# Weight conversion in a pooled-attention and two-MLP kernel: float64 weights turned into two float32 words in 512-word blocks beside the attention, split once and kept

## The chip, the cores and the metric

The kernel runs on one core of a Trainium2 chip. The metric is device time in microseconds (us), the median of several executions; lower is better. The engines are PE (TensorE; PEld is its weight load), DVE (VectorE), ACT (ScalarE) and POOL (GpSimd), which compute, and SP (SyncE), which issues every DMA of this kernel. Each engine works through its own queue in order, so an instruction that waits holds up all that stand behind it on that engine.

## The reference

```python
def _attn_ref(q, k, v):                       # [4, 8, 1152, 64] float32
    q_pool = q.reshape(B, H, S // 2, 2, D).mean(axis=3)
    scores = np.matmul(q_pool, k.transpose(0, 1, 3, 2)) / np.sqrt(D)
    attn = np.exp(scores - np.max(scores, axis=-1, keepdims=True))
    attn = attn / (np.sum(attn, axis=-1, keepdims=True) + 1e-09)
    return np.matmul(attn, v).astype(np.float32)

x = attention output as [2304, 512]           # 4 batches of 576 tokens
h = x @ w_in;  x = np.maximum(0.01 * h, h) @ w_out                      # layer 0
h = x @ w_in2; out = np.where(h > 0, h, np.exp(np.minimum(h, 0)) - 1) @ w_out2   # layer 1
```

`w_in` is [512, 2048] and `w_out` [2048, 512]. The weights arrive as float64, eight bytes each in DRAM; only the results are float32.

## The kernel before, in words

Every float32 operand of a matmul is split into a high word h, rounded to the type that PE multiplies at full rate, and a low word l = x - h; a product is then three matmuls (hh, hl, lh). The helper `psplit` (L258) issues such a split as one instruction for h (L261 on ACT or L263 on DVE) and one subtraction for l (L267 on POOL or DVE).

Attention goes through 16 pairs of heads, four to a batch, nine score tiles to a pair (`attn_pair`). One tile is three 128x384 matmul groups, each followed by one maximum on DVE (L457), so a batch has 108 of these maxima; they serve below as a clock that counts how far the attention has come. Then come exp on ACT (L463), transposes on PE (L475), splits (L261 on ACT, L267 on DVE) and the product with v (L496).

`mlp` does one layer for one batch. For each of 16 feature blocks f it makes h for 128 features (L629, 24 matmuls), the activation on ACT and DVE and a split of the result g (ACT, POOL), and after each four blocks the second product into the accumulators (L667). `load_w` provides the weights of block f as tiles `wi` (3 buffers) and `wo` (6 buffers), each with h and l.

A weight block is 128x512 values, one for `w_in` and one for `w_out` for each f: 64 blocks over both layers. For the first batch of a layer `convert` (L271) makes float32 from the float64 bit pattern in two halves of 256: a load into `cr` (L290), two bit operations on DVE (L293, L296), two conversions on ACT (L299, L301), an addition on POOL (L303) and a last multiplication with a test on DVE (L305) into `wr`. The float32 block is also written to DRAM (L328). For the other three batches `wr` is loaded from that copy (L323). In all four batches `wr` is then split into `wi` or `wo` by ACT (L261) and POOL (L267): 256 splits in all. Waiting for a free `wi` or `wo` happens in ACT's queue.

The order on the engines is set by a list scheduler in the program (`Program.schedule`): every piece of work has an engine, a cost in ns, a rank (the position in the plan; the attention of one tile is one rank, a batch is 36) and its dependences; of what is ready the lowest rank goes first, and the instructions are emitted in the order of the planned starts. `PLAN` gives the rank at which each (batch, layer) MLP starts: 36 and 54 for the first batch, so its MLPs run beside the attention of the second batch, and so on; the last two run with no attention beside them.

## Time and profile before

| | |
|---|---|
| median of 3 runs | 1545.24 us (1543.69 to 1549.79) |
| the profiled execution: its time, its span | 1545.34 us, 1543.5 us |
| PE busy | 92% of the span, 10288 matmuls |
| DVE, ACT, POOL busy | 66%, 69%, 54% |
| DMA | 135.59 MB, 28% of the 16 DMA engines' time |
| granted PE clock | 0.99 of full speed over the span |

The span is what the profile covers; the 1.8 us beside it are outside. Shares are averages over stages with different limits, so each stage is read by itself.

### The profile page before, as it was taken

Reading aid. Unit: us, or ns where it says so; the run is one execution under the profiler, and the core shown is the slowest. Engines: PE = TensorE matmul, PEld = TensorE weight load, DVE = VectorE, ACT = ScalarE, POOL = GpSimd, SP = SyncE. Lnnn points to the kernel's source line nnn. Section 1 sums busy time; section 2 is a strip of 40 time slices with the busy share of each in tenths; the row PEclk is TensorE's granted clock in tenths of the full one; section 3 lists DMA queues with packets and bytes.
Section 4 is the critical chain, followed back from the end, with each engine's and each line's share of the span. In section 5 each row is a group of like instructions: output and inputs, shape, how many; then the busy total and the mean of one; then the engine's idle time right before and its main releaser. Section 6 shows DMA issues by size and latency. Waiting matters only on the chain.

```text
span 1543.5 us, 28953 instructions
## 1 busy us (share of the span) xinstructions
PE 1414.5 (92%) x10288; PEld 1365.2 (88%) x10288; DVE 1011.4 (66%) x2273; ACT 1065.9 (69%) x2901; POOL 830.3 (54%) x840
## 2 busy tenths in 40 slices
PE   5878889888888898999999999999999999899997
...
DVE  6999889899998998556565556645665554124222
...
GB/s 138 99 115 87 40 75 123 121 130 125 126 118 144 130 143 120 74 71 73 67 69 86 79 78 63 74 76 66 71 67 59 55 56 56 93 76 82 69 82 39
DMA packets 82642, 135.59 MB, mean 88 GB/s; under 512 B 8512, under 2 KB 26944, under 8 KB 82496
## 3 DMA queue, kind: packets, MB, share of 16 engines
...
q14 instruction: 65, 0.53, 0.1%
...
## 4 chain that ended last, share of the span: by engine, by line
PE 64%; DVE 21%; ACT 6%; issue 3%; DMA 3%; POOL 2%; SPq 0%; ACTq 0%; POOLq 0%; DVEq 0%
PE h L667 17%; PE h L629 16%; PE s L452 8%; PE o L496 7%; PE t L475 5%; DVE m L457 3%; PE s L629 3%; DVE ct L293 3%; DVE wr L305 3%; DVE ct L296 3%; DVE pt L267 2%; PE s L667 2%; PE t L373 2%; PE t L629 2%; PE t L667 2%
## 5 line engine op out<-in xcount | busy, mean ns | idle before, releaser
L667 PE MATMUL h<-g,wo 128*128 128x288 f32 x2544 | 437.1, 302 | 17.5 <-DVE t L650 7.9
L629 PE MATMUL h<-xs,wi 128*128 128x288 f32 x2520 | 429.2, 305 | 22.9 <-DVE t L650 14.2
L629 PEld LDWEIGHTS h<-xs,wi 128*128 128x128 f32 x2520 | 362.5, 190 | 32.5 <-DVE t L650 20.0
L667 PEld LDWEIGHTS h<-g,wo 128*128 128x128 f32 x2544 | 367.1, 188 | 23.8 <-DVE t L650 9.6
L457 DVE TENSOR_REDUCE m<-s 128x1 f32<-128x384 f32 x432 | 232.2, 550 | 74.4 <-PE s L452 71.6
L261 ACT ACTIVATE pt<-t 128x384 fp32r<-128x384 f32 (+1 forms) x416 | 184.0, 457 | 115.2 <-PE t L475 108.3
L463 ACT ACTIVATE p<-s,m 128x384 f32<-128x384 f32 x432 | 249.5, 588 | 18.3 <-DVE m L459 18.0
L267 DVE TENSOR_TENSOR pt<-t,pt 128x384 fp32r<-128x384 f32 (+1 forms) x416 | 206.8, 509 | 73.3 <-ACT pt L261 71.7
L267 POOL TENSOR_TENSOR g<-t,g 128x288 fp32r<-128x288 f32 x256 | 211.1, 831 | 79.9 <-ACT g L261 75.5
L267 POOL TENSOR_TENSOR wo<-wr,wo 128x512 fp32r<-128x512 f32 x128 | 166.4, 1304 | 137.5 <-ACT wo L261 134.3
L452 PE MATMUL s<-kT,qT 128*128 128x384 f32 x768 | 197.0, 354 | 25.4 <-ACT p L463 24.5
L267 POOL TENSOR_TENSOR wi<-wr,wi 128x512 fp32r<-128x512 f32 x128 | 167.6, 1309 | 91.9 <-ACT wi L261 79.3
L496 PE MATMUL o<-pt,vn 128*128 128x256 f32 (+1 forms) x1152 | 192.5, 303 | 5.5 <-DVE pt L267 3.6
L475 PE MATMUL t<-ident,p 128*128 128x128 f32 x1116 | 181.6, 277 | 12.4 <-DVE pt L267 11.7
L496 PEld LDWEIGHTS o<-pt,vn 128*128 128x128 f32 x1152 | 165.5, 190 | 10.6 <-DVE pt L267 10.2
L475 PEld LDWEIGHTS t<-ident,p 128*128 128x128 f32 x1116 | 139.4, 142 | 22.1 <-DVE pt L267 12.3
L452 PEld LDWEIGHTS s<-kT,qT 128*128 128x128 f32 x768 | 125.5, 192 | 32.2 <-ACT p L463 31.0
L303 POOL TENSOR_TENSOR ct<-ct,cr 128x256 uint32<-128x256 uint32 x128 | 98.8, 774 | 96.7 <-DVE ct L296 29.8
L261 ACT ACTIVATE g<-t 128x288 fp32r<-128x288 f32 x256 | 112.2, 445 | 49.0 <-DVE t L650 28.4
L267 POOL TENSOR_TENSOR vn<-raw,vn 128x576 fp32r<-128x576 f32 x32 | 46.4, 1449 | 174.4 <-ACT vn L261 174.4
L261 ACT ACTIVATE wo<-wr 128x512 fp32r<-128x512 f32 x128 | 80.6, 630 | 78.9 <-PE h L667 47.5
L680 DVE TENSOR_TENSOR acc<-h,acc 128x288 f32<-128x288 f32 x158 | 71.1, 452 | 67.2 <-PE h L667 66.1
(106 smaller groups left out, 2080.0 us busy)
## 6 DMA issues: line engine op xcount, KB each, us to landing
wr<-w SPq DMA_DIRECT2D x192, 256.0 KB, 2.6
cr<-in_moe_w_in_dram SPq DMA_DIRECT2D x64, 256.0 KB, 2.7
cr<-in_moe_w_out_dram SPq DMA_DIRECT2D x64, 256.0 KB, 2.7
w<-wr SPq DMA_DIRECT2D x64, 256.0 KB, 2.4
raw<-in_k_dram SPq DMA_DIRECT2D x32, 288.0 KB, 3.0
raw<-in_v_dram SPq DMA_DIRECT2D x32, 288.0 KB, 3.1
raw<-in_q_dram SPq DMA_DIRECT2D x32, 256.0 KB, 2.9
out_dram<-cr SPq DMA_DIRECT2D x16, 256.0 KB, 2.1
```

Of the source, the lines that this page charges most:

```text
L261: prog.add("ACT", act(n, sbuf=not psum), rank, lambda: A.activation(out=hi(), in_=src(), func=ACTF.Copy), w=[w], r=r)
L267: lambda: eng.tensor_tensor(out=lo(), in0=src(), in1=f32(hi()), op=ALU.subtract),
L293: prog.add("DVE", dve(CW, True), rank, lambda r=r, t=t: V.tensor_scalar(out=t.ap, in0=r[:, :, 1], scalar1=3, scalar2=0x3FFFFFF8, op0=ALU.l ...
L303: prog.add("POOL", pool(CW), rank, lambda t=t, r=r: G.tensor_tensor(out=t.ap, in0=t.ap, in1=r[:, :, 0], op=ALU.add), w=[t], r=[t, (r, 0)])
L452: PE.matmul(out=st[:, 0:384], lhsT=qa(a), rhs=kT[:, 384 * c:384 * c + 384], start=(i == 0), stop=(i == len(seq) - 1))
L457: prog.add("DVE", dve(384), rank - LR, lambda st=st, c=c: V.tensor_reduce(out=m[:, c:c + 1], in_=st[:, 0:384], axis=AX.X, op=ALU.max), w=[ ...
L463: prog.add("ACT", act(384, True), rank - LE, lambda c=c: A.activation(out=p[:, 384 * c:384 * c + 384], in_=banks[c][:, 0:384], func=ACTF.E ...
L475: PE.transpose(out=t[:, i, :], in_=p[:, (3 * c + i) * 128:(3 * c + i + 1) * 128], identity=ident)
L496: PE.matmul(out=o[:, 0:n], lhsT=vn[:, c, :], rhs=pt[th][:, a, c % 3, :], start=(c == 3 * ORDER[0] and a == 0), stop=(c == 3 * ORDER[2] + 2 ...
L629: PE.matmul(out=h[:, 0:HB], lhsT=wi[:, a, c, :], rhs=xs[c][:, e, cols], start=(c == 0 and a == 0 and e == 0), stop=(c == DC - 1 and a == 1))
L667: PE.matmul(out=y[:, 0:HB], lhsT=w[f][1][:, a, d * 128:(d + 1) * 128], rhs=g[f][:, e, cols], start=(f % FC == 0 and a == 0 and e == 0), st ...
L680: prog.add("DVE", dve(HB), rank - HURRY, lambda y=y, a_=a_, cols=cols: V.tensor_tensor(out=a_[:, cols], in0=y[:, 0:HB], in1=a_[:, cols], o ...
```

## The change

`convert` works on 512 words at a time, without the `ct` and `cm` tiles: the intermediate words lie in the tile that becomes the result, and the absolute value (L301) is taken in place. A new function `prepare_w` converts one block into `ws` (2 buffers), splits it there once into h (ACT) and l (POOL), and writes both to DRAM, 512 KB a block. `CONV` gives this stream ranks of its own: layer 0 from 14 to 48, layer 1 from 48 to 66. `load_w` no longer computes: `wi` and `wo` are filled by a DMA from the kept h and l, in all four batches, also in the first. The planner's cost of a group of three MLP matmuls rises from 369 to 399. `cr` buffers are 512 words of eight bytes; `store` uses them too. `SPILL` is empty, so the branches that ask for it do nothing; `PLAN`'s new column holds the same 18 as before.

```diff
-    CW = 256
+    CW = 512
     CB = 2
-    CLEAD = 3
     FC = 4
     GB = 5
     WIB = 3
     WOB = 6
-    WRB = 4
+    WSB = 2
+    CONV = ((14, 48), (48, 66))
+    SPILL = ()
...
-    PLAN = ((0, 0, 36, 0), (0, 1, 54, 0), (1, 0, 72, 0), (1, 1, 90, 0),
-            (2, 0, 108, 0), (2, 1, 126, 0), (3, 0, 144, 1), (3, 1, 162, 1))
+    PLAN = ((0, 0, 36, 18, 0), (0, 1, 54, 18, 0), (1, 0, 72, 18, 0), (1, 1, 90, 18, 0),
+            (2, 0, 108, 18, 0), (2, 1, 126, 18, 0), (3, 0, 144, 18, 1), (3, 1, 162, 18, 1))
...
-            t = sb("ct", [128, CW], U32, CB)
-            mag = sb("cm", [128, CW], F32, CB)
+            t = lambda n=n: f32(dst[:, 1, n:n + CW]).bitcast(U32)
...
             prog.add("DVE", dve(CW, True), rank, lambda r=r, t=t: V.tensor_scalar(
-                out=t.ap, in0=r[:, :, 1], scalar1=3, scalar2=0x3FFFFFF8,
-                op0=ALU.logical_shift_left, op1=ALU.bitwise_and), w=[t], r=[(r, 1)])
+                out=t(), in0=r[:, :, 1], scalar1=3, scalar2=0x3FFFFFF8,
+                op0=ALU.logical_shift_left, op1=ALU.bitwise_and), w=[(dst, n)], r=[(r, 1)])
             prog.add("DVE", dve(CW), rank, lambda r=r, t=t: V.scalar_tensor_tensor(
-                out=t.ap, in0=r[:, :, 1], scalar=0xC0000000, in1=t.ap,
-                op0=ALU.bitwise_and, op1=ALU.bitwise_or), w=[t], r=[(r, 1), t])
+                out=t(), in0=r[:, :, 1], scalar=0xC0000000, in1=t(),
+                op0=ALU.bitwise_and, op1=ALU.bitwise_or), w=[(dst, n)], r=[(r, 1), (dst, n)])
             prog.add("ACT", act(CW, sbuf=True), rank, lambda r=r: A.activation(
                 out=r[:, :, 0], in_=r[:, :, 0], func=ACTF.Copy, scale=2.0 ** -29), w=[(r, 0)], r=[(r, 0)])
-            prog.add("ACT", act(CW, sbuf=True), rank, lambda r=r, mag=mag: A.activation(
-                out=mag.ap, in_=r[:, :, 1].bitcast(F32), func=ACTF.Abs), w=[mag], r=[(r, 1)])
+            prog.add("ACT", act(CW, sbuf=True), rank, lambda r=r: A.activation(
+                out=r[:, :, 1].bitcast(F32), in_=r[:, :, 1].bitcast(F32), func=ACTF.Abs),
+                w=[(r, 1)], r=[(r, 1)])
             prog.add("POOL", pool(CW), rank, lambda t=t, r=r: G.tensor_tensor(
-                out=t.ap, in0=t.ap, in1=r[:, :, 0], op=ALU.add), w=[t], r=[t, (r, 0)])
-            prog.add("DVE", dve(CW), rank, lambda n=n, t=t, mag=mag: V.scalar_tensor_tensor(
-                out=dst[:, n:n + CW], in0=mag.ap, scalar=MIN_HI, in1=t.ap.bitcast(F32),
-                op0=ALU.is_ge, op1=ALU.mult), w=[(dst, n)], r=[t, mag])
+                out=t(), in0=t(), in1=r[:, :, 0], op=ALU.add), w=[(dst, n)], r=[(dst, n), (r, 0)])
+            prog.add("DVE", dve(CW), rank, lambda t=t, r=r: V.scalar_tensor_tensor(
+                out=t().bitcast(F32), in0=r[:, :, 1].bitcast(F32), scalar=MIN_HI, in1=t().bitcast(F32),
+                op0=ALU.is_ge, op1=ALU.mult), w=[(dst, n)], r=[(dst, n), (r, 1)])
...
+    def prepare_w(rank, layer, w_in, w_out, f, i):
+        src = block(layer, w_in, w_out, f, i)
+        ws = sb("ws", [128, 2, 512], F32R, WSB)
+        x = lambda: f32(ws[:, 1])
+            convert(rank, ws, src)
+        prog.add("ACT", act(512, sbuf=True), rank, lambda: A.activation(
+            out=ws[:, 0], in_=x(), func=ACTF.Copy), w=[(ws, "h")], r=[ws])
+        prog.add("POOL", pool(512), rank, lambda: G.tensor_tensor(
+            out=ws[:, 1], in0=x(), in1=f32(ws[:, 0]), op=ALU.subtract), w=[ws], r=[ws])
+        kp = kept[layer, f, i] = Buf(lambda: dram.tile([128, 1024], F32, name=f"w{layer}_{f}_{i}"))
+        prog.add("SP", 60, rank, lambda: nc.sync.dma_start(
+            out=kp.ap, in_=f32(ws.ap).rearrange("p a n -> p (a n)")), w=[kp], r=[ws])
+
     def load_w(rank, layer, w_in, w_out, f):
-
-        src = (w_in[:, f * 128:(f + 1) * 128].rearrange("(c p) f -> p c f", p=128),
-               w_out[f * 128:(f + 1) * 128, :])
-        rs = [sb("wr", [128, 512], F32, WRB) for _ in range(2)]
-        for i, r in enumerate(rs):
-            if w_in.dtype == F32:
-                view = (lambda r=r: r.ap.rearrange("p (c n) -> p c n", c=DC)) if i == 0 else lambda r=r: r.ap
-                prog.add("SP", 60, rank - 1.5, lambda i=i, view=view: nc.sync.dma_start(
-                    out=view(), in_=src[i]), w=[r])
-            elif (layer, f, i) in kept:
-                kp = kept[layer, f, i]
-                prog.add("SP", 60, rank - 1.5, lambda r=r, kp=kp: nc.sync.dma_start(
-                    out=r.ap, in_=kp.ap), w=[r], r=[kp])
-            else:
-                convert(rank - CLEAD, r, src[i])
-                kp = kept[layer, f, i] = Buf(lambda i=i: dram.tile([128, 512], F32, name=f"w{layer}_{f}_{i}"))
-                prog.add("SP", 60, rank, lambda r=r, kp=kp: nc.sync.dma_start(out=kp.ap, in_=r.ap), w=[kp], r=[r])
         wi = sb("wi", [128, 2, DC, 128], F32R, WIB)
         wo = sb("wo", [128, 2, DM], F32R, WOB)
-        psplit(rank - 0.5, WH, WL, lambda: wi[:, 0].rearrange("p c n -> p (c n)"),
-               lambda: wi[:, 1].rearrange("p c n -> p (c n)"), lambda: rs[0].ap, 512, (wi, 0), [rs[0]])
-        psplit(rank - 0.5, WH, WL, lambda: wo[:, 0], lambda: wo[:, 1], lambda: rs[1].ap, 512, (wo, 0), [rs[1]])
+        prog.add("SP", 60, rank - 1.5, lambda: nc.sync.dma_start(
+            out=f32(wi.ap).rearrange("p a c n -> p (a c n)"), in_=kept[layer, f, 0].ap), w=[wi], r=[kept[layer, f, 0]])
+        prog.add("SP", 60, rank - 1.5, lambda: nc.sync.dma_start(
+            out=f32(wo.ap).rearrange("p a n -> p (a n)"), in_=kept[layer, f, 1].ap), w=[wo], r=[kept[layer, f, 1]])
...
-                    prog.add("PE", 3 * 123, rank + step * hf / 2, lambda h=h, c=c, cols=cols: mm(h, c, cols),
+                    prog.add("PE", 3 * 133, rank + step * hf / 2, lambda h=h, c=c, cols=cols: mm(h, c, cols),
...
-            o = sb("cr", [128, DM], F32, CB)
+            o = sb("cr", [128, 2 * DM], F32, CB)
...
+    ws_ = ((moe_w_in, moe_w_out), (moe2_w_in, moe2_w_out))
+    for layer, (first, last) in enumerate(CONV):
+        for n in range(2 * FT):
+            prepare_w(first + (last - first) * n / (2 * FT), layer, *ws_[layer], n // 2, n % 2)
+    for b, layer, at, width, wide in PLAN:
         tags = [(u, size[u]) for u in ("h" * HBUFS + ("t" * TB + "s" * SBUFS if wide else ""))]
-        w = ((moe_w_in, moe_w_out), (moe2_w_in, moe2_w_out))[layer]
-        xin[b] = mlp(at + WLAG, span / 2, b, layer, xin[b], *w, tags)
+        w = ws_[layer]
+        xin[b] = mlp(at + WLAG, width, b, layer, xin[b], *w, tags)
```

Three places in the order. First DVE, somewhat over half way through the second batch's attention. `cr` holds the loaded float64 words, `ct`/`wr` (before) and `ws` (after) the converted ones, `t` with a number is an activation, `pt` the split of the attention weights. Before, from the 171st maximum to the next:
```order
L293 TENSOR_SCALAR ct<-cr 128x256
L267 TENSOR_TENSOR pt<-t,pt 128x3x128
L642 TENSOR_TENSOR t_5432<-h,t_5432 128x288
L296 SCALAR_TENSOR_TENSOR ct<-cr,ct 128x256
L305 SCALAR_TENSOR_TENSOR wr<-cm,ct 128x256
L642 TENSOR_TENSOR t_5475<-h,t_5475 128x288
L263 CAST qn<-qs 128x512
L293 TENSOR_SCALAR ct<-cr 128x256
L305 SCALAR_TENSOR_TENSOR wr<-cm,ct 128x256
L642 TENSOR_TENSOR t_5512<-h,t_5512 128x288
L296 SCALAR_TENSOR_TENSOR ct<-cr,ct 128x256
L457 TENSOR_REDUCE m<-s 128x1
```
The changed kernel, up to the same maximum (its L293, L296 and L306 are the L293, L296 and L305 of before; L655 is L642, L465 is L457):
```order
L293 TENSOR_SCALAR ws<-cr 128x512
L296 SCALAR_TENSOR_TENSOR ws<-cr,ws 128x512
L655 TENSOR_TENSOR t_5159<-h,t_5159 128x288
L268 TENSOR_TENSOR pt<-t,pt 128x3x128
L655 TENSOR_TENSOR t_5185<-h,t_5185 128x288
L293 TENSOR_SCALAR ws<-cr 128x512
L296 SCALAR_TENSOR_TENSOR ws<-cr,ws 128x512
L655 TENSOR_TENSOR t_5227<-h,t_5227 128x288
L264 CAST qn<-qs 128x512
L306 SCALAR_TENSOR_TENSOR ws<-cr,ws 128x512
L465 TENSOR_REDUCE m<-s 128x1
```
The conversion's instructions are half as many and twice as wide, and they stand at the same kind of place between attention and activation. Counted over the whole queue, 22 of before's 128 L293 stand ahead of the 109th maximum (the end of the first batch's attention), the next behind the 120th and the last behind the 222nd; of after's 64, 21 stand ahead of the 109th (20 of the L306), the next directly behind it, and the last L293 and L306 behind the 201st and the 204th.

Second SP, its queue of DMA issues in the same batch, with the semaphores that each waits for (DMAHW: an earlier DMA; `cr` loads, `w` the kept blocks). Before:
```order
L290 DMA cr<-in_moe_w_out_dram 128x512 [waits DMAHW2_49,DMAHW7_49,Activation_49,Pool_49]
L349 DMA raw<-in_v_dram 128x576 [waits DMAHW3_49]
L290 DMA cr<-in_moe_w_out_dram 128x512 [waits DMAHW0_49,Activation_49,Pool_49]
L328 DMA w_0_0_5284<-wr 128x512 [waits DVE_49]
L290 DMA cr<-in_moe_w_in_dram 128x2x256 [waits DMAHW2_49,DMAHW6_49,Activation_49,Pool_49]
L290 DMA cr<-in_moe_w_in_dram 128x2x256 [waits DMAHW4_49,Activation_49,Pool_49]
L328 DMA w_0_1_5389<-wr 128x512 [waits DVE_49]
L290 DMA cr<-in_moe_w_out_dram 128x512 [waits DMAHW1_49,DVE_49,DMAHW6_49,Activation_49,Pool_49]
L290 DMA cr<-in_moe_w_out_dram 128x512 [waits DMAHW7_49,Activation_49,Pool_49]
L328 DMA w_1_0_5530<-wr 128x512 [waits DMAHW3_49,DVE_49]
```
The changed kernel, a little earlier in the plan, where layer 0 is at its end:
```order
L340 DMA wo<-w_6_1_1936 128x1024 [waits DMAHW2_49,PE_49]
L332 DMA w_14_1_3720<-ws 128x1024 [waits Pool_49]
L340 DMA wo<-w_7_1_2168 128x1024 [waits DMAHW4_49,PE_49]
L340 DMA wo<-w_8_1_2385 128x1024 [waits DMAHW5_49,PE_49]
L290 DMA cr<-in_moe_w_in_dram 128x4x256 [waits DMAHW7_49,DMAHW6_49,DVE_49]
L357 DMA raw<-in_v_dram 128x576
L340 DMA wo<-w_9_1_2644 128x1024 [waits DMAHW0_49,PE_49]
L332 DMA w_15_0_3812<-ws 128x1024 [waits DMAHW1_49,Pool_49]
L338 DMA wi<-w_7_0_2024 128x1024 [waits DMAHW2_49,PE_49]
L290 DMA cr<-in_moe_w_out_dram 128x1024 [waits DMAHW3_49,DVE_49]
L338 DMA wi<-w_8_0_2374 128x1024 [waits DMAHW4_49,PE_49]
L290 DMA cr<-in_moe_w_in_dram 128x4x256 [waits DMAHW6_49,DMAHW5_49,DVE_49]
```
Loads of `wo` and `wi` that wait for PE now stand in one queue with the `cr` loads and the writes of the conversion; before, that wait was ACT's.

Third PE, in the last MLP (batch 3, layer 1), where the fourth block's `wi` is first used; numbers tell the buffers apart, and the first row is the last use of the buffer that this `wi` takes over. Before:
```order
L629 MATMUL h_19337<-xs_19211,wi_19024 128x288 x3
L629 MATMUL s_19283<-xs_19211,wi_19165 128x288 x3
L667 MATMUL t_19376<-g_19342,wo_19048 128x288 [waits DVE_49]
L667 MATMUL t_19376<-g_19342,wo_19048 128x288 [waits Pool_49]
L667 MATMUL t_19376<-g_19342,wo_19048 128x288
L629 MATMUL s_19391<-xs_19176,wi_19374 128x288 [waits Activation_49]
L629 MATMUL s_19391<-xs_19176,wi_19374 128x288
L629 MATMUL s_19391<-xs_19176,wi_19374 128x288 [waits Pool_49]
```
The changed kernel:
```order
L642 MATMUL h_18133<-xs_18005,wi_17836 128x288 x3
L642 MATMUL s_18075<-xs_18005,wi_17927 128x288 x3
L680 MATMUL t_18172<-g_18130,wo_17865 128x288 [waits DMAHW1_49,DVE_49]
L680 MATMUL t_18172<-g_18130,wo_17865 128x288 [waits Pool_49]
L680 MATMUL t_18172<-g_18130,wo_17865 128x288
L642 MATMUL s_18180<-xs_17968,wi_18156 128x288 [waits DMAHW0_49]
L642 MATMUL s_18180<-xs_17968,wi_18156 128x288 x2
```
The matmuls are the same and so is their distance, six matmuls from the last use to the next; the first use waited for ACT and POOL and now waits for a DMA.

## Rows read from the trace of the kernel before

**Rows 1.** The page's first lines: the span; each engine's busy time, share and instructions; and the busy tenths of PE and DVE in 40 slices of 38.6 us.
```profile
span 1543.5 us, 28953 instructions
PE 1414.5 (92%) x10288; PEld 1365.2 (88%) x10288; DVE 1011.4 (66%) x2273; ACT 1065.9 (69%) x2901; POOL 830.3 (54%) x840
PE   5878889888888898999999999999999999899997
DVE  6999889899998998556565556645665554124222
```

**Rows 2.** Seven stretches of the span. Columns: stretch and length in us; busy us and instructions of PE, PEld, DVE, ACT and POOL; granted PE clock; share of the DMA engines; GB/s.
```profile
0.00:195.00 195.00, 149.33 (x1001) 135.22 (x1001) 166.49 (x402) 165.07 (x470) 82.99 (x92) 0.97 0.30 95
195.00:240.00 45.00, 40.57 (x281) 38.20 (x282) 39.65 (x98) 35.69 (x105) 23.40 (x26) 0.96 0.23 75
240.00:590.00 350.00, 306.37 (x2166) 286.02 (x2165) 326.69 (x691) 268.63 (x752) 226.64 (x238) 1.00 0.41 132
590.00:675.00 85.00, 76.62 (x547) 74.35 (x546) 52.79 (x117) 58.33 (x157) 44.39 (x44) 0.96 0.29 89
675.00:900.00 225.00, 224.49 (x1705) 223.47 (x1704) 133.56 (x310) 158.73 (x431) 116.57 (x113) 1.00 0.23 68
900.00:1250.00 350.00, 343.96 (x2599) 340.47 (x2598) 205.88 (x469) 246.54 (x668) 175.80 (x171) 1.00 0.23 69
1250.00:1543.50 293.50, 273.12 (x2000) 267.50 (x1998) 86.38 (x191) 132.93 (x325) 160.55 (x160) 0.99 0.24 71
```

**Rows 3.** The chain that ended last, by line, first of 195 to 600 us, then of 600 to 1250 us.
```profile
by line: DVE ct L296 9.5%; DVE wr L305 9.5%; DVE ct L293 9.3%; DVE m L457 7.3%; issue 7.3%; PE h L629 6.2%; DVE pt L267 5.3%; PE h L667 4.4%; DMA cr<-in_moe_w_out_dram 3.5%; DMA cr<-in_moe_w_in_dram 3.1%; PE s L452 3.0%; PE o L496 2.4%; POO
by line: PE h L667 28.5%; PE h L629 27.4%; PE s L452 11.6%; PE o L496 10.5%; PE t L475 9.5%; PE t L373 2.7%; DVE xs L263 1.5%; issue 0.8%; DMA out_dram<-cr 0.7%; DMA wr<-w 0.7%; DVE xs L267 0.6%; DVE t L650 0.5%; ACT t L645 0.5%; ACT cr L70
```

**Rows 4.** DVE's three conversion instructions: count, duration in ns as minimum/median/maximum, first and last start in us, form.
```profile
L293 DVE TENSOR_SCALAR ct<-cr x128: 273/294/1514, 7.7 to 589.7; 128x256 uint32<-128x256 uint32 x128
L296 DVE SCALAR_TENSOR_TENSOR ct<-cr,ct x128: 403/426/1661, 9.4 to 591.1; 128x256 uint32<-128x256 uint32 x128
L305 DVE SCALAR_TENSOR_TENSOR wr<-cm,ct x128: 402/417/1685, 12.6 to 593.3; 128x256 f32<-128x256 f32 x128
```

**Rows 5.** From the timeline, two conversion instructions of DVE and the POOL instruction nearest to each. Columns: start us, length us, instruction.
```profile
389.57 0.81 POOL L267 TENSOR_TENSOR g<-t,g 128x288 fp32r<-128x288 f32 x1 [0.84 <-ACT g L261]
389.39 0.28 DVE L293 TENSOR_SCALAR ct<-cr 128x256 uint32<-128x256 uint32 x1
391.06 1.47 POOL L267 TENSOR_TENSOR wo<-wr,wo 128x512 fp32r<-128x512 f32 x1
391.30 1.51 DVE L305 SCALAR_TENSOR_TENSOR wr<-cm,ct 128x256 f32<-128x256 f32 x1
```

**Rows 6.** Groups of instructions by line and form: total busy us, mean ns of one | idle us of the engine before them and what ended it.
```profile
L267 DVE TENSOR_TENSOR pt<-t,pt 128x384 fp32r<-128x384 f32 x328 | 177.5, 551 | 56.7 <-ACT pt L261 55.5
L267 DVE TENSOR_TENSOR pt<-t,pt 128x192 fp32r<-128x192 f32 x88 | 29.3, 351 | 16.6 <-ACT pt L261 16.2
L299 ACT ACTIVATE cr<-cr 128x256 uint32<-128x256 uint32 x128 | 56.3, 440 | 23.0 <-DMA cr<-in_moe_w_out_dram 15.0 <-DMA cr<-in_moe_w_in_dram 6.7 <-POOL wi L267 0.9
L301 ACT ACTIVATE cm<-cr 128x256 f32<-128x256 f32 x128 | 55.2, 433 | 3.4 <-DVE wr L305 3.4
L261 ACT ACTIVATE wi<-wr 128x512 fp32r<-128x512 f32 x128 | 80.7, 630 | 5.0 <-DVE wr L305 3.6 <-DMA wr<-w 1.4
L267 POOL TENSOR_TENSOR wi<-wr,wi 128x512 fp32r<-128x512 f32 x128 | 167.6, 1309 | 91.9 <-ACT wi L261 79.3 <-DVE wr L305 3.0 <-PE s L452 2.4
```

**Rows 7.** The busy DVE time and count of L293, then of L296, then of L305, in 0 to 195 and 195 to 590 us (clock, DMA share and GB/s behind them).
```profile
0.00:195.00 195.00, 11.95 (x22) 0.97 0.30 95
195.00:590.00 395.00, 55.48 (x106) 0.99 0.39 125
0.00:195.00 195.00, 12.78 (x22) 0.97 0.30 95
195.00:590.00 395.00, 68.59 (x105) 0.99 0.39 125
0.00:195.00 195.00, 9.18 (x20) 0.97 0.30 95
195.00:590.00 395.00, 73.85 (x106) 0.99 0.39 125
```

**Rows 8.** DMA issues: what, count, KB each, median us from issue to landing.
```profile
wr<-w SPq DMA_DIRECT2D x192, 256.0 KB, 2.6
w<-wr SPq DMA_DIRECT2D x64, 256.0 KB, 2.4
raw<-in_k_dram SPq DMA_DIRECT2D x32, 288.0 KB, 3.0
```

**Rows 9.** The last stage. First two of ACT's waits in 1254 to 1543 us (total us, times, longest); then three pieces of the timeline in the last MLP, around the place that the PE order above shows: start us, length us, instruction, [idle before, what ended it].
```profile
ACT wo L261 <- PE h L667: 33.1, 4, 15.8
ACT wo L261 <- PE s L667: 20.4, 4, 11.8
1435.43 0.55 PE L629 MATMUL s<-xs,wi 128*128 128x288 f32 x3
1438.01 1.28 POOL L267 TENSOR_TENSOR wi<-wr,wi 128x512 fp32r<-128x512 f32 x1 [2.25 <-ACT wi L261]
1439.34 0.19 PEld L629 LDWEIGHTS s<-xs,wi 128*128 128x128 f32 x1 [0.94 <-POOL wi L267]
```

35 lines of the change are left out of this document (27 added, 8 removed).

## Prediction

> **What bounds the kernel now.** I began with the page's first lines: PE is busy 92% of 1543.5 us, so little can be won where PE is full, and the slices show that it isn't full before 620 us, while DVE stands at 8 and 9 tenths there and falls to 5 and 6 after [rows 1]. The table of stretches makes this exact [rows 2]. From 675 to 900 us PE is busy 224.49 of 225 us and does 1705 matmuls, 132 ns each: that is the rate of a saturated PE here, and I use it as a floor for any stretch with attention and MLP mixed. From 240 to 590 us PE does 2166 matmuls, whose floor is 2166 x 0.132 = 286 us, but takes 350; DVE is busy 326.69 us, 93.3%. The chain says who holds the end: between 195 and 600 us its three largest lines are L296, L305 and L293, the conversion on DVE, with 28% together; between 600 and 1250 us it is PE's matmuls [rows 3]. So three stages matter: A, 0 to 195 us, attention alone, where DVE (166 us) and ACT (165 us) are the fullest; B, 195 to 590 us, attention, MLP and conversion, bound by DVE; and the rest, bound by PE, with a last stage from 1250 us in which 2000 matmuls (264 us) take 293.5 us. What the change saves on ACT and POOL after 590 us is worth nothing unless PE waited for it.
>
> **The conversion on DVE.** The medians of L293, L296 and L305 at 256 words are 294, 426 and 417 ns, 1.137 us for a half block, 2.27 for a block; the maxima are 1.5 to 1.7 us [rows 4]. The timeline shows what lies between: L293 alone took 0.28 us, but the L305 that starts at 391.30 behind a POOL subtraction of 391.06 to 392.53 ends at 392.81, together with it and 0.28 us later [rows 5]. DVE is held until POOL's instruction ends. All of it, from the busy time, was 11.95 + 12.78 + 9.18 = 33.9 us in A for some 21 halves, and 55.48 + 68.59 + 73.85 = 197.9 us in B for some 106 [rows 7]: per half 1.59 and 1.87 us, of which 0.45 and 0.73 are waiting, 0.24 us an instruction in B.
>
> At 512 words no row exists. Doubling gives 2.27 us a block as the upper end without waits. A fixed part doesn't double: DVE's split of `pt` takes 551 ns at 384 elements and 351 at 192 [rows 6], so 1.04 ns an element over 151 ns. With 151 ns taken off once an instruction, a block is 2.27 - 0.45 = 1.82 us; I take that. For waiting I take the same mean per instruction, half as many instructions: 0.73 a block in B, 0.45 in A; the ends are none and double. So a block costs 2.55 us in B (1.82 to 3.3) and 2.27 us in A.
>
> The Trainium skill, "SBUF — State Buffer", section "Who interferes with whom", says that a DVE instruction with two SBUF inputs or in a two-port mode and a GpSimd instruction exclude each other for the whole instruction, so a wait should grow with POOL's instruction, and the conversion's addition doubles in width. By that rule 0.24 us would become about 0.30 as the mean POOL instruction of B grows, and B's conversion would cost some 8 us more than by the row's mean; no run here shows it yet, and I stay with the row.
>
> **Stage B.** By the order, 43.5 of the 64 blocks are converted behind the first batch's attention, up to the 204th maximum; before it was 53 blocks, up to the 222nd at 590 us. So conversion fills (204 - 108)/(222 - 108) = 84% of B. DVE's other work in B is 39.65 + 326.69 - 197.9 = 168 us [rows 2, 7]; 84% is 141.5, and 43.5 x 2.55 = 111 us of conversion make 252.5, at the 93.3% that DVE reached 271 us. PE's floor in B is (281 + 2166) x 0.132 = 323 us, of which 84% is 271 too. Two engines that are equally full hold each other up, so I don't take 323 for B but 345, a share of 94% for PE where DVE-bound B had 82% and pure PE stages 98 to 100%. B shrinks by 50 us; the ends are 72 (the floor) and 20 (waits double, so 3.3 us a block: (141.5 + 143.5)/0.933 = 305, + 52 for the rest, + 18 of friction = 375).
>
> **Stage A.** It gets 20.5 blocks where it had 11. DVE: 20.5 x 2.27 = 46.5 against 33.9, +12.6 us. ACT: before 11 x 4 x 0.437 = 19.2 us, and a few first splits, at most nine of 0.63 us, since three `wi` and six `wo` are all there are; after, three passes over 512 words, each like the 0.63 us of the `wi` split [rows 6], so 20.5 x 1.9 = 39: +14 to +20 us. Both engines are idle 29 us of 195 [rows 2]. If all of it fits in the gaps A is unchanged, if none does it grows by 18; I take +12. At the very start DVE's first conversion stands ahead of the first q work and now waits for a load of 512 KB: +1.
>
> **The loads of `wi` and `wo`.** 192 loads of 256 KB become 256 loads of 512 KB, the write too doubles; DMA stands at 23 to 41% of its engines [rows 2], so the traffic itself has room. Landing: 256 KB take 2.6 us, 288 KB 3.0 [rows 8]; 512 KB lie between 2.6 (nothing for size) and 2.6 + 8 x 0.4 = 5.8; I take 4.0, nearer the low end, since a small part of the 2.6 can be transfer. With 0.3 us for PE's signal and SP's issue that is 4.3 us from the last use of a buffer to its next. While attention runs, the order leaves at least 57 matmuls between the two, 57 x 0.132 = 7.5 us: hidden. In the last stage there are places with 3, 6, 12 and 18 matmuls. At the one with 6 the last use ended by 1435.43 and the first use came with POOL's split at 1438.01, its third matmul at 1439.34 [rows 9], so the DMA, at 1439.7, costs half a microsecond to 1.6 more than split and waiting did; four such places make some +5 us. Against it ACT no longer stands still for a free `wo` (33.1 and 20.4 us in the last stage [rows 9]) with activations queued behind it, and POOL's splits are gone: -3. Net +2, between -8 and +12.
>
> **What is put at nothing.** ACT loses 192 splits of 0.63 us and POOL 192 of 1.31 us [rows 6], nearly all after 590 us, where PE is the bound. The wait for a free `wo` moves from ACT into SP's queue, where attention's loads and the `cr` loads stand behind it; it costs nothing as long as those are early. The planner's 399 ns for three MLP matmuls is the 3 x 132 of the trace; what the order gains from it I can't price and leave out.
>
> **The sum**, against the profiled execution's 1545.3 us (0.1 above the median): -50 (B) + 12 + 1 (A) + 2 (last stage) = 1510.
>
> **Rivals.** *More.* DVE's waits fall further, as POOL has fewer instructions in B, and friction stays small: B near its floor, 330, and A +5: 1545 - 65 + 5 + 2 = 1487. For it: DVE was the only full engine of B. Against: both are full for 84% of it.
>
> *The stream of two buffers (slower).* A block holds its `ws` from L293 until its write has landed: 0.44 + 0.69 + 1.31 + 0.69 on DVE and POOL (the addition taken like the split), 0.63 + 1.31 for the split, and 3.2 to 4 for the write (2.4 us at 256 KB [rows 8]), 9 us without one wait. At five hand-overs between engines that are 65 to 93% busy, one microsecond each gives 14 us, two buffers one block per 7 us, 43.5 blocks 305 us, and DVE, in order, waits at L293 with the maxima and activations behind it. B is then 305 + 52 = 357, total 1522. From a hold of 16 us on, B is 348 + 52 = 400 and the end is beyond 1553, slower. SP pushes that way: `cr` loads stand behind loads that wait for PE, as the order of SP shows. Against: at 0.24 us an instruction the waits are shorter than what I allow, and `ws` gaps in the order are long in A.
>
> *HBM under load.* The Trainium skill, "DMA: Bandwidth & Descriptors", section "Latency and other measured facts", gives an HBM access 0.2 us on average and 2 us at high load; this trace has landings of 2.4 to 3.0 us in the median [rows 8], and no run here shows twice the traffic. In rows' terms, each landing at the upper 5.8 us, the four places of the last stage cost +12 instead of +2 and the total is 1520; a hold of `ws` that is 2 us longer brings the slower case nearer.
>
> *Nothing.* What B gains A loses (+18), B shrinks by only 20: 1545 - 20 + 18 + 2 = 1545.
>
> **How the numbers follow.** Forecast 1495 to 1530: 0.53. More gain, under 1495: 0.14. Little gain, 1530 to 1537: 0.09. Within 0.5% (1537.5 to 1553, about what a measurement of this kernel tells from no change): 0.10. Slower, the two buffers: 0.14. So faster 0.76, same 0.10, slower 0.14. The range 1478 to 1550 leaves out 0.03 below and 0.16 above.
>
> **What would show it.** Right: the last conversion ends near 530 us instead of 593; L293, L296 and the last step have medians near 0.44, 0.69 and 0.69 us and means 0.2 to 0.3 above; PE is busy over 92% of the stretch between; A ends near 207 us by the 108th maximum; PE waits for `wi` DMAs at a few places of the last stage only. Wrong: DVE idle at L293 for `cr` or for the kept write; PE waiting for `wi` or `wo` in the MLPs of the first batch; A longer by over 20 us.

## The result and the profile after

The changed kernel takes 1563.72 us in the median of 4 runs (1559.51 to 1568.68), the kernel before, run beside it, 1544.47 (1543.64 to 1549.79): a ratio of 1.012, interval 1.008 to 1.016. It is slower by 19 us, 1.2%; 1510 were forecast. The profiled execution took 1566.78 us, span 1565.0, so the two traces are 21.5 us apart.

The first lines of the page of after, against [rows 1]; below them the tenths of the granted PE clock:

```profile
span 1565.0 us, 28067 instructions
PE 1427.9 (91%) x10288; PEld 1383.7 (88%) x10288; DVE 944.9 (60%) x2081; ACT 959.3 (61%) x2581; POOL 579.6 (37%) x584
PE   5787878888889899899999999999999999799898
DVE  6989998776678765645556555645566553123222
PEclk9988999998999999999999999999999999899999
```

DVE, ACT and POOL lost the work that they were to lose: 66, 107 and 251 us. In the kernel before DVE's row showed 8 and 9 from the 7th to the 15th slice; now it shows 6 to 8, and PE's row is no better for it.

To see where the time went, both traces are cut at the 108th, the 222nd and the last of the 432 maxima on DVE (L465, before L457). The first cut is the end of the first batch's attention, the second lies six maxima, two score tiles, behind the end of the second batch's, the third is the end of all attention. The stretches are called A, B, C and the last stage. First before, then after; columns as in [rows 2]:

```profile
0.00:193.50 193.50, 148.64 (x997) 134.77 (x998) 165.09 (x399) 163.65 (x466) 82.07 (x92) 0.97 0.30 95
193.50:587.50 394.00, 345.12 (x2433) 322.17 (x2432) 365.24 (x785) 304.00 (x855) 248.95 (x261) 0.99 0.38 124
587.50:1259.50 672.00, 656.97 (x4932) 649.95 (x4931) 400.17 (x912) 473.43 (x1280) 346.09 (x336) 0.99 0.24 72
1259.50:1543.50 284.00, 263.73 (x1933) 258.35 (x1931) 80.94 (x180) 124.85 (x302) 153.24 (x153) 0.99 0.23 69
```
```profile
0.00:208.50 208.50, 155.16 (x1001) 140.84 (x1001) 183.24 (x399) 177.81 (x475) 110.33 (x102) 0.94 0.51 171
208.50:597.50 389.00, 338.04 (x2319) 320.18 (x2320) 292.25 (x590) 276.07 (x713) 216.40 (x190) 0.95 0.61 208
597.50:1271.50 674.00, 663.98 (x4996) 657.23 (x4995) 388.06 (x910) 410.35 (x1154) 184.31 (x207) 0.99 0.35 119
1271.50:1565.00 293.50, 270.69 (x1976) 265.45 (x1974) 81.33 (x185) 95.11 (x241) 68.53 (x86) 0.96 0.39 134
```

Stage A is 15 us longer, B 5 us shorter, C 2 and the last stage 9.5 longer. In B DVE fell from 93% busy to 75%, PE stayed at 87 to 88%, and it did 114 matmuls fewer, which the later stages had to make up.

What DVE and ACT waited for from DMAs between 208 and 560 us of after (conversion's part of B; total us, times, longest):

```profile
DVE ws L293 <- DMA w<-ws: 33.6, 19, 5.3
ACT cr L299 <- DMA cr<-in_moe_w_in_dram: 16.1, 9, 2.9
ACT cr L299 <- DMA cr<-in_moe_w_out_dram: 8.7, 7, 3.0
```

PE waits for no DMA in B. Of its 51 us of idle time there 44 end with an instruction of DVE; the two longest rows:

```profile
PE t L483 <- DVE pt L268: 14.5, 13, 2.9
PE h L642 <- DVE t L655: 8.7, 6, 2.4
```

The landings of after (count, KB, median us from issue), against [rows 8]:

```profile
wi<-w SPq DMA_DIRECT2D x128, 512.0 KB, 3.4
wo<-w SPq DMA_DIRECT2D x128, 512.0 KB, 5.2
w<-ws SPq DMA_DIRECT2D x64, 512.0 KB, 3.8
out_dram<-cr SPq DMA_DIRECT2D x16, 256.0 KB, 3.6
```

One of those waits, from the timeline of after: start us, length us, instruction, [idle before, what ended it].

```profile
295.98 0.33 SPq L332 DMA_DIRECT2D w<-ws  x1
299.52 0.46 DVE L655 TENSOR_TENSOR t<-h,t 128x288 f32<-128x288 f32 x1 [1.09 <-ACT t L653]
303.38 0.43 DVE L293 TENSOR_SCALAR ws<-cr 128x512 uint32<-128x512 uint32 x1 [3.39 <-DMA w<-ws]
303.72 0.55 DVE L465 TENSOR_REDUCE m<-s 128x1 f32<-128x384 f32 x1
305.39 0.45 DVE L655 TENSOR_TENSOR t<-h,t 128x288 f32<-128x288 f32 x1
305.89 0.66 PE L642 MATMUL h<-xs,wi 128*128 128x288 f32 x3 [2.32 <-DVE t L655]
```

The write of a block, issued at 295.98, releases its buffer 7.4 us later. DVE's next instruction is L293 on that buffer: 3.39 us idle. Behind it stand a maximum, two more conversion steps and the activation L655, and PE waits 2.32 us for the last. The Trainium skill, "PSUM — Partial Sum Buffer", section "Engine vs sequencer instructions", calls the queues of ACT, DVE and POOL strict FIFO (first in, first out). The trace agrees for DVE: nothing on it passes the waiting L293.

### The profile page after: what moved, and what is told of

Same layout as the page of the kernel before. It is cut to its first block, busy times and chain, and to the rows that moved or that the text cites. A ratio compares the mean times of both kernels' runs of the same rounds, so it can differ in the third digit from the quotient of the medians.

```text
span 1565.0 us, 28067 instructions
## 1 busy us (share of the span) xinstructions
PE 1427.9 (91%) x10288; PEld 1383.7 (88%) x10288; DVE 944.9 (60%) x2081; ACT 959.3 (61%) x2581; POOL 579.6 (37%) x584
## 4 chain that ended last, share of the span: by engine, by line
PE 66%; DVE 12%; DMA 10%; ACT 5%; POOL 3%; issue 3%; SPq 0%; ACTq 0%; DVEq 0%; POOLq 0%
PE h L680 18%; PE h L642 17%; PE s L460 8%; PE o L504 7%; PE t L483 5%; DMA w<-ws 5%; PE s L642 3%; PE s L680 2%; DVE m L465 2%; DVE pt L268 2%; PE t L680 2%; DMA out_dram<-cr 2%; PE t L381 2%; PE t L642 2%; DVE ws L296 2%
## 5 line engine op out<-in xcount | busy, mean ns | idle before, releaser
L642 PE MATMUL h<-xs,wi 128*128 128x288 f32 x2520 | 448.9, 310 | 22.7 <-DVE t L663 9.4
L680 PE MATMUL h<-g,wo 128*128 128x288 f32 x2544 | 442.9, 303 | 10.1 <-DVE t L663 6.3
L642 PEld LDWEIGHTS h<-xs,wi 128*128 128x128 f32 x2520 | 373.8, 195 | 29.9 <-DVE t L663 13.1
L465 DVE TENSOR_REDUCE m<-s 128x1 f32<-128x384 f32 x432 | 231.8, 551 | 70.2 <-PE s L460 66.5
L471 ACT ACTIVATE p<-s,m 128x384 f32<-128x384 f32 x432 | 249.1, 587 | 11.9 <-DVE m L467 11.4
L460 PEld LDWEIGHTS s<-kT,qT 128*128 128x128 f32 x768 | 129.3, 197 | 43.4 <-ACT p L471 40.9
L483 PEld LDWEIGHTS t<-ident,p 128*128 128x128 f32 x1116 | 140.1, 142 | 26.0 <-DVE pt L268 18.5
L268 POOL TENSOR_TENSOR vn<-raw,vn 128x576 fp32r<-128x576 f32 x32 | 46.5, 1454 | 227.0 <-ACT vn L262 216.7
L304 POOL TENSOR_TENSOR ws<-ws,cr 128x512 uint32<-128x512 uint32 x64 | 84.8, 1325 | 104.8 <-DVE ws L296 45.2
L329 POOL TENSOR_TENSOR ws<-ws 128x512 fp32r<-128x512 f32 x64 | 86.4, 1353 | 68.1 <-ACT ws L327 67.8
L655 DVE TENSOR_TENSOR t<-h,t 128x288 f32<-128x288 f32 x105 | 47.6, 455 | 88.9 <-ACT t L653 88.3
L471 ACT ACTIVATION_READ_ACCUMULATOR p<-s,m 128x1 f32 x432 | 92.1, 213 | 0.0
```

The source lines that it names most:

```text
L268: lambda: eng.tensor_tensor(out=lo(), in0=src(), in1=f32(hi()), op=ALU.subtract),
L304: prog.add("POOL", pool(CW), rank, lambda t=t, r=r: G.tensor_tensor(out=t(), in0=t(), in1=r[:, :, 0], op=ALU.add), w=[(dst, n)], r=[(dst, ...
L329: prog.add("POOL", pool(512), rank, lambda: G.tensor_tensor(out=ws[:, 1], in0=x(), in1=f32(ws[:, 0]), op=ALU.subtract), w=[ws], r=[ws])
L460: PE.matmul(out=st[:, 0:384], lhsT=qa(a), rhs=kT[:, 384 * c:384 * c + 384], start=(i == 0), stop=(i == len(seq) - 1))
L465: prog.add("DVE", dve(384), rank - LR, lambda st=st, c=c: V.tensor_reduce(out=m[:, c:c + 1], in_=st[:, 0:384], axis=AX.X, op=ALU.max), w=[ ...
L471: prog.add("ACT", act(384, True), rank - LE, lambda c=c: A.activation(out=p[:, 384 * c:384 * c + 384], in_=banks[c][:, 0:384], func=ACTF.E ...
```

## The experiments

Four theories of why B did not shrink. *Loop of two buffers*: two `ws` buffers, each taken up for some 16 us, allow one block per 8 us. *Traffic*: 236 MB instead of 136 delay every transfer. *Order*: the planner fixes each engine's order with 2500 ns for any transfer, and so puts instructions ahead of others although their transfers of 512 KB land later. *Clock*: the granted clock, 0.95 in B, stretches PE's work.

All runs of the changed kernel; "waits" are those of DVE and ACT for DMAs from 208 to 560 us as above. A, B, C and the last stage are cut at the maxima, and "PE idle" is PE's idle time in B; these are of the profiled execution, in us. The time is the median, the ratio that to the kernel before on the same chip.

| run | waits DVE + ACT | A, B, C, last | PE idle | us | ratio (95%) |
|---|---|---|---|---|---|
| after | 33.6 + 24.8 | 208, 390, 673, 294 | 51 | 1563.7 | 1.012 (1.008–1.016) |
| wob5 | 36.5 + 24.3 | 208, 391, 673, 304 | 55 | 1577.9 | 1.021 (1.018–1.023) |
| wob5_ws3 | 34.1 + 26.6 | 220, 383, 670, 305 | 51 | 1581.8 | 1.023 (1.020–1.026) |
| cw256_ws3 | 37.1 + 42.2 | 213, 413, 668, 292 | 64 | 1587.8 | 1.028 (1.025–1.031) |
| nowrite | 16.3 + 18.5 | 223, 369, 671, 292 | 43 | 1558.7 | 1.008 (1.005–1.010) |
| a123 | 34.5 + 18.0 | 202, 395, 674, 295 | 57 | 1576.9 | 1.020 (1.015–1.026) |
| latwrite | 6.2 + 38.6 | 212, 396, 667, 294 | 54 | 1570.6 | 1.016 (1.014–1.019) |
| latload | 34.3 + 24.8 | 207, 390, 670, 296 | 55 | 1567.1 | 1.014 (1.010–1.018) |
| latcr | 32.4 + 1.0 | 203, 389, 668, 294 | 56 | 1558.6 | 1.010 (1.007–1.013) |
| latconv | 10.7 + 1.8 | 211, 370, 667, 295 | 37 | 1543.0 | 0.999 (0.997–1.001) |
| lat4 | 16.1 + 8.8 | 218, 367, 667, 294 | 36 | 1548.1 | 1.001 (0.999–1.003) |
| lat55 | 7.2 + 4.0 | 209, 365, 662, 297 | 34 | 1535.0 | 0.993 (0.991–0.995) |
| lat55_storeact | 6.2 + 3.1 | 211, 366, 671, 297 | 34 | 1547.0 | 1.001 (0.999–1.003) |
| lat8 | none | 203, 346, 677, 299 | 20 | 1526.1 | 0.989 (0.986–0.992) |
| lat8_store4 | none | 204, 344, 670, 291 | 20 | 1509.4 | 0.976 (0.975–0.978) |
| lat12 | none | 211, 332, 795, 300 | 36 | 1635.5 | 1.056 (1.054–1.059) |

Three things help to read it. B goes with PE's idle time in it (but for lat12, where B holds less work). The sum of the two waits is no price, since DVE and ACT can stand at the same time: where ACT's 24.8 us are gone and DVE's stay (latcr), B stays at 389. And executions of one kernel lie up to 17 us apart (a123: 1568.5 to 1585.8); the intervals of nowrite, a123, latwrite, latload and latcr overlap that of after, so none of these five is told from it by its time.

### More buffers, smaller blocks, no writes

```diff
-    WOB = 6            # wob5
+    WOB = 5
-    WSB = 2            # wob5_ws3: this too
+    WSB = 3
```


> The changed kernel with five wo buffers in place of six, the control for the next run. Every theory: the stretch from the 108th to the 222nd maximum on DVE stays at the changed kernel's 389 us (within 8), the whole between 1560 and 1585 us, since one buffer less makes wo loads start later wherever PE is near its work.

> Five wo buffers and three ws buffers in place of two. Theory 'loop of two buffers' (a ws buffer is held 16 us from the first DVE step to the landing of its 512 KB write, and two of them pace the stream at 8 us a block): the pace becomes 16/3 = 5.3 us, under what DVE needs anyway, and the stretch from the 108th to the 222nd maximum falls from 389 to 345-360 us; the whole is 25 to 45 us under the control with five wo buffers. Theory 'traffic and queue order' (the doubled writes and loads on SP's queue delay one another): a third buffer takes no byte and no place off the queue; the stretch stays at 380 us or above and the whole within 10 us of the control. Theory 'clock' (the granted clock of 0.94 in this stretch stretches PE's own work): the same as traffic, no gain over 10 us.

A wo buffer less costs 14 us. The third ws buffer gives nothing back: +4 us on the control, B 383. L293's starts show that the loop theory's faster pace did not come: blocks 20 to 60 came every 7.97 us in after and come every 7.87 here, so the time from one L293 to the next on the same buffer is three times the pace (23.5 us) where it was twice (16.1). The stall moved:

```profile
DVE ws L293 <- DMA cr<-in_moe_w_out_dram: 16.7, 6, 5.2
DVE ws L293 <- DMA cr<-in_moe_w_in_dram: 10.1, 7, 4.8
DVE ws L293 <- DMA w<-ws: 7.3, 3, 4.4
```

```diff
-    CW = 512           # cw256_ws3, with WSB = 3
+    CW = 256
```


> Conversion steps at 256 words instead of 512 (two halves to a block, as in the kernel before), whose smaller cr buffers make room for the third ws buffer, with six wo buffers. Theory 'loop of two buffers': stretch 108th to 222nd maximum 350 to 370 us (some 6 us over the previous run's for the fixed cost of twice as many DVE steps), whole 1520 to 1540 us. Theories 'traffic and queue order' and 'clock': 380 us or above, whole 1555 to 1575 us. Where cr's two buffers pace the stream in place of ws (halves come one by one), 370 to 390 us.

A miss for every theory: B 413, with 79 us of waits, all for cr loads, of which there are now two to a block.

```diff
+        if f:          # nowrite, in prepare_w ahead of the kept write
+            return
```


> The changed kernel with 60 of its 64 kept writes left out: only the blocks of f = 0 are written, and every wi and wo load reads those (so the output isn't the reference's; the traffic of the loads is unchanged). A ws buffer is then held to the end of POOL's subtraction, about 9 to 10 us of the 16. Theory 'loop of two buffers': two buffers give 5 us a block; stretch 108th to 222nd maximum 345 to 360 us, whole 1520 to 1540 us. Theory 'traffic and queue order': the writes are 30 MB of 64 MB moved for weights; with half of the added traffic gone half of the loss goes, 365 to 375 us. Theory 'clock': 380 us or above.

B falls by 21 us to 369, inside the range of "traffic"; but with the writes DVE's waits for them go too (from 33.6 to 5.0 us), so this run does not tell bytes from waits. The first 108 maxima take 223 us, and 5 of 19 us come back. DVE now waits 11.3 us for cr loads.

### The planner's number

```diff
-    LATENCY = {"PE": 200, "SP": 2500, ...
+    LATENCY = {"PE": 200, "SP": 4000, ...   # lat55: 5500, lat8: 8000, lat12: 12000
```


> The changed kernel, planner's latency of a transfer 4000 ns instead of 2500 (the changed kernel's transfers of 512 KB landed after medians of 3.4 to 5.2 us, the kernel before's of 256 KB after 2.4 to 2.7); it alters the order on every engine and nothing else. Theory 'order': DVE's fixed order puts conversion steps where their buffer or load isn't there yet, and what stands behind them (activations, maxima, low parts) makes PE wait; with a truer latency PE's waits for DVE in the stretch 208 to 597 us fall from 45 us to 20 to 30, whole 1540 to 1552 us. Theory 'loop of two buffers': the order can't shorten a hold; 1558 to 1568 us. Theory 'traffic': 1558 to 1568 us.

> As the run with 4000, with 5500 ns (the wo loads' median and the landing of a write with its wait). Theory 'order': 1535 to 1552 us, no worse than with 4000; the late wi and store places of the last stage shrink by 3 us too. The other theories: 1558 to 1568 us, or longer where the planner now starts the stream's steps later and the first MLP behind them.

The order alone, with every byte and buffer as it was, takes off 16 and 29 us, as "order" forecast. PE's idle time in B falls from 51 to 36 and 34 us, while B holds 2330 and 2353 matmuls after 2321, so no work has left it. Only the last stage did not shrink as expected; with 5500 it is 297 us instead of 294. Waits for DMAs in 208 to 560 us of the run with 5500:

```profile
DVE ws L293 <- DMA w<-ws: 7.2, 8, 2.4
ACT cr L299 <- DMA cr<-in_moe_w_in_dram: 3.2, 3, 1.4
ACT cr L299 <- DMA cr<-in_moe_w_out_dram: 0.8, 1, 0.8
```

> The changed kernel with the planner's old cost of three matmuls, 3 x 123 in place of 3 x 133. If the new cost is what delays the MLP's matmuls against the attention (119 fewer matmuls between the 108th and the 222nd maximum), the whole falls by 5 to 15 us; every other theory: within 6 us of 1563.

A miss for every theory: by the medians the old cost is 13 us slower, but the two intervals overlap. So the new cost (3 x 133) is no part of the loss.

> The kernel before (conversion in halves inside the first batch of a layer, four wr buffers) with the one part 'split once, keep h and l': the first batch splits into wi and wo as it did and writes those 512 KB, the other batches load wi and wo from there, with no split. Theory 'stream' (the loss sits in the conversion's stream of two buffers, or in where it stands in DVE's order): no loss before the 222nd maximum (585 to 592 us), and in all 1535 to 1550 us, with 3 to 8 us lost in the last stage to loads of 512 KB that land late. Theory 'traffic': 512 KB in place of 256 KB for each load and write costs here as it does there, 1555 to 1570 us.

The one part "kept as h and l" in the kernel before: 1547.6 us, ratio 1.002 (1.000 to 1.004). Its 222nd maximum comes at 584 us (588 before), although B moves 162 GB/s instead of 124; the last stage loses 12 us, more than the 3 to 8 expected, with PE waiting 5.6 us for wi and 5.3 behind a store. So keeping h and l in 512 KB costs in the last stage only. What B failed to win must lie in the stream, which this run leaves out.

### Which transfer

Each of these adds 3000 ns for one kind of transfer in the planner's table.

> The changed kernel, the planner told 3000 ns more for the 64 kept writes alone (2500 as before for every load). Theory 'order, write': DVE's 33.6 us of waits for a ws buffer whose write hasn't landed (208 to 597 us) are the stall that makes PE late, so this alone gives most of what 5500 for all gave (29 us): 1535 to 1548 us, that wait under 12 us. Theory 'order, loads' (late cr, wi or wo loads matter most): 1555 to 1566 us.

> The same 3000 ns for the 256 wi and wo loads alone. Theory 'order, write': no gain before the 222nd maximum (592 to 600 us), at most some 5 us in the last stage where wi lands late; 1556 to 1566 us. Theory 'order, loads': 1540 to 1552 us.

> The same 3000 ns for the 64 cr loads alone. Theory 'order, write': a part at most, as DVE's waits for cr are short in the changed kernel, 1555 to 1566 us, DVE's wait for the write still over 25 us. Theory 'order, loads': 1540 to 1552 us.

A miss: no kind alone gave it. Corrected writes let DVE go (6.2 us left) and left ACT standing longer, the first two lines (latwrite). Corrected cr loads did the reverse, the other two (latcr, where the lines of the kernel are one further down):

```profile
ACT cr L299 <- DMA cr<-in_moe_w_out_dram: 21.6, 10, 4.3
ACT cr L299 <- DMA cr<-in_moe_w_in_dram: 17.0, 11, 4.2
```
```profile
DVE ws L294 <- DMA w<-ws: 32.4, 17, 5.4
ACT cr L300 <- DMA cr<-in_moe_w_in_dram: 0.5, 1, 0.5
```

> The changed kernel, 3000 ns more for the cr loads and the kept writes both, every other transfer at 2500. Theory 'two waits' (DVE for the kept writes and ACT for the cr loads are one loop; each corrected alone left or raised the other: 6 and 39 us with the write corrected, 32 and 1 us with the load, against 34 and 25): both fall under 10 us between 208 and 560 us, and the whole to 1535 to 1548 us. Rival 'all loads': the k, q, v, wi and wo loads had to be corrected too, or a chance order did it; 1553 to 1568 us.

Both together: the waits are 10.7 and 1.8 us, the time is 1543 us, 21 of the 29 us of lat55. B falls by 20 us and PE's idle time in it by 14.

> The kernel before with the planner's latency of a transfer at 5500 ns. If the changed kernel lost because 2500 is untrue for its transfers of 512 KB, the kernel before, whose transfers of 256 KB take 2.4 to 2.7 us, gains nothing: 1540 to 1556 us. If 5500 is a better order for either kernel (a gain that has nothing to do with this change), it gains the like of 29 us: 1515 to 1530 us.

A miss for both: the kernel before loses 39 us by 5500 (1583.5 us, ratio 1.025, 1.022 to 1.028), so 5500 is no better order as such. B falls there to 345, but with 2085 matmuls in it instead of 2429: the planner has put part of the first MLPs behind it, and the next 210 maxima take 760 us instead of 672.

> The kernel before with 1200 ns for every transfer, half of the 2.4 to 2.7 us that its 256 KB transfers take. Theory 'waits': the same fault as the changed kernel has by 2500, so DVE's and ACT's waits for transfers between 193 and 587 us grow by 10 us or more, and the whole by 5 to 25 us. Rival (the order is a lottery, and any number may help or harm): no such growth of these waits, or a whole at 1545 us or less with it.

1570.0 us, ratio 1.016 (1.014 to 1.018), B 407 after 394. The waits between 193 and 587 us, first of the kernel before, then of this run:

```profile
DVE ct L293 <- DMA cr<-in_moe_w_in_dram: 1.8, 3, 1.2
DVE ct L293 <- DMA cr<-in_moe_w_out_dram: 1.6, 2, 0.8
ACT cr L299 <- DMA cr<-in_moe_w_out_dram: 11.3, 12, 2.4
ACT cr L299 <- DMA cr<-in_moe_w_in_dram: 2.7, 3, 1.3
```
```profile
DVE ct L293 <- DMA cr<-in_moe_w_out_dram: 8.9, 14, 1.4
DVE ct L293 <- DMA cr<-in_moe_w_in_dram: 6.5, 12, 1.0
ACT cr L299 <- DMA cr<-in_moe_w_in_dram: 33.8, 31, 3.3
ACT cr L299 <- DMA cr<-in_moe_w_out_dram: 23.5, 34, 2.5
```

As theory "waits" forecast: told half of what its transfers take, the kernel before waits 72.7 us where it waited 17.4, and loses 24 us, 13 of them in B. That is the changed kernel's fault, made in the kernel before.

> The changed kernel with 8000 ns for every transfer, above what nearly all of them take. Theory 'two waits': no DMA wait is left to remove beyond 5500 (11 us of DVE and ACT between 208 and 560 us), so no further gain over 6 us; the stream's steps are placed later than need be, 1530 to 1560 us. Rival 'the later the better' (the number helps by delaying conversions, whatever they wait for): a further gain of 8 us or more, under 1527 us.

A further 9 us: more than "two waits" allowed (6), and inside the range of its rival, which the next run tests. No row of DVE or ACT waits for a DMA in the stretch. Its B:

```profile
203.50:548.00 344.50, 324.31 (x2345) 311.45 (x2345) 287.72 (x589) 275.03 (x711) 210.84 (x186) 0.99 0.65 224
```

Against after's B it is 44.5 us shorter: 30.8 us of PE's idle time and 13.7 us of its busy time, with 26 matmuls more. It moves 224 GB/s instead of 208, so traffic as such falls as the cause. The clock is 0.99 where after's B had 0.95, and only the order was changed, so the lower clock is not the change's own. What lowered it is not shown: B of the kernel before has 49 us of PE's idle time too, at 0.99.

Nor does the pace of the stream set B. Blocks come every 8.15 us here, no faster than in after, and the last L293 stands later (572.6 against 549.7 us). What changed is how long DVE stands for a buffer. From a block's L293 to the landing of its write 11.9 us pass in the mean of blocks 20 to 60 (14.9 in after), and from that landing to the next L293 on the buffer 4.4 us (1.2 in after, where 20 of 40 started within 0.3 us of the landing). The step comes when its buffer is free, and nothing stands in line behind it.

> The changed kernel with 12000 ns for every transfer. Theory 'waits' (the number helps by taking DVE and ACT off transfers that haven't landed; at 8000 ns 1 us of that is left): no further gain, 1522 to 1545 us. Rival 'the later the better': 1519 us or less.

A miss for both, and "the later the better" falls. B is 332 us, but with 2063 matmuls in it instead of lat8's 2352: as in the kernel before with 5500, part of the first MLPs now lies behind it, and the next 210 maxima take 795 us.

So what is shown of the 44 us that lie between the B of after and of lat8 is this: correcting the number for conversion's own transfers alone takes off 20 (latconv), for all transfers 24 (lat55), and the waits go with it. How much of the last step, from 5500 to 8000, is waits (11 us of DVE and ACT were left) and how much another order, is not told apart.

### The last stage

PE does 43 matmuls more than before in its 293.5 us (43 x 0.132 = 5.7 us); its idle time is 22.8 us after 20.3. There is one long stall. The timeline of after at the change to the last batch:

```profile
1334.21 1.16 SPq L340 DMA_DIRECT2D wo<-w  x2
1335.46 0.38 SPq L733 DMA_DIRECT2D out_dram<-cr  x1
1335.93 0.91 SPq L340 DMA_DIRECT2D wo<-w  x2
1341.11 0.60 ACT L728 ACTIVATE cr<-h 128x512 f32<-128x512 f32 x1 [4.22 <-DMA out_dram<-cr]
1341.76 1.06 PE L722 MATMUL h<-ident,acc 128*64 128x128 f32 x4 [4.16 <-ACT cr L728]
1345.16 5.11 PE L642 MATMUL h<-xs,wi 128*128 128x288 f32 x22 [2.34 <-ACT cr L728]
```

Four loads of 512 KB are in flight with the store, which lands after 5.5 us and the next one after 7.5; ACT's next copy waits for its cr buffer, PE for the copy. In the kernel before the stores there landed after 2.0 to 2.5 us, and PE's two waits were short:

```profile
1322.17 0.62 PE L701 MATMUL h<-ident,acc 128*64 128x128 f32 x4 [0.64 <-ACT cr L707]
1324.08 3.46 PE L629 MATMUL h<-xs,wi 128*128 128x288 f32 x24 [1.28 <-ACT cr L707]
```

```diff
-            prog.add("SP", 60, at, ... nc.sync.dma_start(     # lat55_storeact
+            prog.add("ACT", 60, at, ... nc.scalar.dma_start(
```


> The changed kernel with 5500 ns for every transfer, and the 20 stores of the output issued from ACT's queue behind the copy that fills them, so that they no longer stand behind wo loads on SP's queue. Theory 'queue order in the last stage' (four 512 KB wo loads issued ahead of the store make it land late, and the next copy into that cr buffer and PE behind it wait 6.9 and 1.8 us in the run with 5500): those waits fall to 2 us or less, whole 1526 to 1531 us. Rival 'landing time' (the transfers share the same 16 engines whichever queue issues them): the waits stay, 1532 to 1539 us.

The queue is not it. The store from ACT's queue lands after 3.5 us in the median (3.7 in lat55), and after 6.0 to 6.2 at the batch change:

```profile
out_dram<-cr ACTq DMA_DIRECT2D x16, 256.0 KB, 3.5
```

PE still waits there, 5.2 and 4.0 us, and the whole is 12 us longer, outside both ranges. Of this 9 us lie between the 222nd and the last maximum, and the trace says where: at the two earlier changes of the output's batch PE now waits 7.8 us for the copies, and in lat55 it did not wait for one. Why the copies come later there is open. The Trainium skill, "DMA: Bandwidth & Descriptors", section "Issuing engines are not separate DMA queues", says that transfers run on the same 16 engines and interleave whoever issues them. The landing, no earlier from ACT's queue, agrees.

```diff
+            if t % 2:                                         # lat8_store4
+                o = sb("ws", [128, 2, DM], F32R, WSB)
```


> The run with 8000 ns, and every second store of the output goes through a ws buffer (idle by then) in place of a cr buffer, so that four buffers in place of two stand between the copy on ACT and the landing of its store. Theory 'buffer reuse': ACT's waits of 6.1 and 1.2 us for a store's landing at the last batch change, and PE's behind them, fall under 1 us; whole 1517 to 1521 us. Rival 'landing time' (PE waits for wi at that place anyway): no gain over 3 us, 1523 to 1528 us.

More than expected, 16.7 us under lat8. In the span of lat8 PE waited 6.1 and 1.9 us for the copies, here nowhere; that is 8 us, the last stage's own gain (299 to 291). The stores land no earlier (up to 8.8 us at the batch change), so it is the buffers that hide them. Of the rest, 6.7 us lie between the 222nd and the last maximum: 2.7 us of PE's idle time (12.8 to 10.1) and 4 us of its busy time, with the same 4961 matmuls; the cause is open. This version is faster than both kernels, 2.4% under the kernel before.

## Why the prediction was wrong

- **Stage B** is the step that failed: 345 forecast, 390 measured. DVE's work was right: 111 us of conversion were counted on and 107 measured. The wait inside an instruction was 0.22 us in the mean, near the 0.24 taken over from the kernel before and not the 0.30 that POOL's longer instructions would have made of it. The three steps have the durations forecast (minimum/median/maximum):

```profile
L293 DVE TENSOR_SCALAR ws<-cr x64: 367/427/1649, 8.5 to 549.7; 128x512 uint32<-128x512 uint32 x64
L296 DVE SCALAR_TENSOR_TENSOR ws<-cr,ws x64: 674/693/1868, 9.6 to 550.2; 128x512 uint32<-128x512 uint32 x64
L306 DVE SCALAR_TENSOR_TENSOR ws<-cr,ws x64: 630/684/1900, 13.8 to 553.5; 128x512 f32<-128x512 f32 x64
```

  What failed is the friction between PE's floor of 323 us and "345, a share of 94% for PE". It was put at 22 us, and the only waiting that was worked out from rows is that inside DVE's instructions, 0.73 us a block [rows 7]. Idle time of DVE and ACT at conversion's own transfers had no term. It was 33.6 us of DVE and 24.8 of ACT, and PE stood idle for 51 us of B, 31 more than in lat8, where those waits are gone. The prediction had one fact at hand and the kernel the other: a landing of 512 KB was put at 4.0 us, and the planner made the order with 2500 ns; the two were never set against each other. DVE idle at L293 for the kept write was named as a sign of being wrong, and it is what came.

  With the waits taken away by the order (lat8) B is 344.5 us with PE busy 94%. That it meets the forecast so closely is in part luck: it holds 2345 matmuls where 2447 were forecast, 13 us less at 0.132, and each takes 138 ns. The whole is still 1526 and not 1510, as A (+9), C (+5) and the last stage (+14.5) are longer than in the kernel before.
- **"It costs nothing as long as those are early"**, of the cr loads on SP's queue: they weren't, ACT's 24.8 us are theirs. Taken away alone they gave B nothing (latcr); with DVE's waits corrected too they count (B is 396 us in latwrite and 370 in latconv).
- **The rival of two buffers** had the sign, one block per 8 us, B near 400 and the time beyond 1553, and a wrong cause: a third buffer gained nothing, and lat8 is fast with blocks as far apart. From L293 to the landing a block took 14.9 us, where 9 without a wait were worked out. Its real part was the half sentence "DVE, in order, waits at L293 with the maxima and activations behind it".
- **Stage A**: +13 forecast, +15 measured. Right, though not firmly: conversion on DVE took 50.8 us there (46.5 forecast), and other orders of the same kernel put the end of A between 202 us (a123) and 218 us (lat4).
- **The last stage**: +2 forecast, +9.5 measured. The late wi loads were there, 3.1 us of PE's time; the store of the output, a transfer that the change doesn't touch, was left out, as was the MLP work that B left over.
- **HBM under load**: landings did grow (3.4 to 5.2 us, within the 2.6 to 5.8 given), also where the size stayed the same (stores of 256 KB from 2.1 to 3.6 us); whether the HBM is what is slow, no run shows. And 1520 for that was far too small, since it was priced at four places of the last stage and not in the order.
